# K^T p in four column strips, and the chain's single-column matmuls spread over more slots

## The chip, the cores and the metric

The kernel runs on one core of one Trainium2 chip. The metric is the device time of one execution in microseconds (us). Engines are named as in the profile: PE (TensorE) does the matmuls and PEld its weight loads, DVE is VectorE, ACT is ScalarE, POOL is GpSimd, SP is SyncE, which here only issues loads.

## What is computed

One transformer layer at decode (a single query per sequence, batch 2, width 512), forward and backward. A conditioning vector gives six shift, scale and gate vectors; layer norm, attention over a cache of 8192 keys in 32 heads of 128, then a gated feed-forward block of width 1376. Outputs are the layer's result and the gradients of all inputs but one. The parts that matter for the time:

```python
scores = jnp.einsum('bhqd,bhkd->bhqk', q, k_cache) * Dh ** (-0.5)
p = _softmax(scores, axis=-1)
o = jnp.einsum('bhqk,bhkd->bhqd', p, v_cache)
...
_out, _vjp = jax.vjp(_f, A_x, A_k_cache, A_v_cache, A_wq, A_wo, B_w1, B_w3, B_w2, c, w_mod)
```

K and V are bf16, 2 MB each for each of the 64 (batch, head) pairs. Their gradients are two outer products per head: dV = p dO^T and dK = ds q^T, where ds = p (V dO - sum). Each is 2 MB per head to be written. The gradient of q is the sum over keys of ds times K. The kernel gets it from two things that it collects while K and V are on the chip: the 128x128 matrix V^T diag(p) K, and the vector K^T p. The vector is what the change computes in another way.

## The kernel before

**Two kinds of job.** A job takes eight slots of a schedule that is written out by hand (`at(slot, place, f)`; at the end, all slots are run through in order, and within a slot by place). Jobs of kind A, one for each of 64 heads, load K and V and collect the forward part. Jobs of kind C, one for each head, load V a second time and write dV and dK. C jobs of a batch can only start when the whole batch's A jobs and the chain behind them (output projection, feed-forward, its backward, dO) are through. So A jobs of batch 0 run alone first, 32 of them; then the chain of batch 0 is laid over A jobs of batch 1; then A jobs of batch 1 and C jobs of batch 0 alternate; then come the chain of batch 1 and the rest of the C jobs.

**An A job.** K of a head is two tiles of 1 MB ("half" tiles, 128 partitions x 32 blocks x 128), V as well. In each of eight slots:

- `a_t`: eight 128x128 transposes of K into a PSUM tile `tp` (L353), copied to SBUF by ACT (L358) or, for two of eight groups, by DVE (L356).
- `a_s`, two slots later: eight single-column matmuls of the transposed blocks with q (L373), the scores.
- After eight groups: maximum, exponential (`a_exp`, L391) into `E2`, 64 bf16 values on each partition, each twice.
- `a_scale`, in four parts: DVE multiplies K by p (L399) into `ek`, 128 columns, and POOL puts p itself into a 129th (L401); POOL also keeps p for the C job (L403).
- `a_m`, from slot 15 of the job on (`MOFF`), eight slots: for each of the 64 blocks of 128 keys, one matmul of V with `ek`, 129 columns (L414: V^T diag(p) K and V^T p), and one of K with p, a single column (L416: K^T p). Both accumulate in one PSUM tile, over 64 blocks. K and V are each loaded as weights, 128x128.
- `a_free`: half of K and half of V go back together after four of the eight groups, the others after eight.
- `a_evac`: ACT copies the matrix out, DVE the two vectors into `OK`.

In steady state three A jobs overlap, so a slot holds eight transposes, eight score columns, eight L414 and eight L416.

**A C job.** `c_t` and `c_s` transpose V and multiply with dO (L353 and L951); DVE makes the outer products (L974) into half tiles, which POOL writes out (L979).

**Buffers and loads.** All 1 MB tiles, loads, outputs and large weights, come from one pool of 21. Loads are sorted by the slot that needs them (`want`) and issued on SP in that order, each as soon as a tile is released (`release`, `pump`). SP runs its issues in order, each waiting for its own tile.

**PSUM.** Eight banks: four for `tp`, two for scores and small results (`scr` hands out columns of them), two for L414's sums and other wide results.

**The chain** (`steps_chain`) is a list of steps, each with the number of slots to the next; `lay` puts them on slots as tasks, which come last in a slot. Its matmuls with one column: the output projection (L702, 4 x 32), `proj` for w1 and w3 (L756, 44 each) and w2 (L792, 44). Its 23 slots and the planner's rules set which slot the first C job gets (`TC = E0 + 5`, where `E0` is the end of the chain).

Of the kernel before, what the change touches and what calls it, by code (L numbers as in the profile page):

```python
# [8 lines left out]
BF16 = mybir.dt.bfloat16  # L9
F32 = mybir.dt.float32  # L10
ALU = mybir.AluOpType
ACT = mybir.ActivationFunctionType
AX = mybir.AxisListType
# [4 lines left out]
def kernel(  # L18
# [26 lines left out]
    nc = tc.nc  # L45
    P = 128
    B, Sq, D = A_x.shape
    assert Sq == 1 and B == 2
    _, H, Sk, Dh = A_k_cache.shape
# [3 lines left out]
    NC = D // P  # L53
    KK = Sk // P
    MC = MD // P
    FC = (F + P - 1) // P
    FL = F - (FC - 1) * P
    NHD = B * H
# [8 lines left out]
    HK = KK // 2  # L67
# [4 lines left out]
    def hb(i):  # L72
        return i // H, i % H
# [4 lines left out]
    cst = ctx.enter_context(tc.tile_pool(name="cst", bufs=1))  # L78
# [3 lines left out]
    ktp = ctx.enter_context(tc.tile_pool(name="ktp", bufs=4))  # L82
    ekp = ctx.enter_context(tc.tile_pool(name="ekp", bufs=3))
    hw = ctx.enter_context(tc.tile_pool(name="hw", bufs=2))
    tps = ctx.enter_context(tc.tile_pool(name="tps", bufs=4, space=bass.MemoryType.PSUM))
    sps = ctx.enter_context(tc.tile_pool(name="sps", bufs=2, space=bass.MemoryType.PSUM))
    mps = ctx.enter_context(tc.tile_pool(name="mps", bufs=2, space=bass.MemoryType.PSUM))

    HN = HK * P

# [9 lines left out]
    def mtps():  # L100
        return mps.tile([P, 512], F32, name="m_ps", tag="m_ps")

    identb = cst.tile([P, P], BF16, name="identb")
# [4 lines left out]
    nc.vector.tensor_scalar(nident[:], identb[:], -SCL, None, ALU.mult)  # L108
    eps_t = cst.tile([P, 1], F32, name="eps_t")
    nc.vector.memset(eps_t[:], EPS)  # L110

    rsum = cst.tile([P, NHD], F32, name="rsum")
    OK = cst.tile([P, NHD, 2], F32, name="OK")
# [11 lines left out]
    for nm, ap in (("c", c), ("x", A_x.rearrange("b s d -> (b s) d")),  # L125
                   ("dy", grad_out.rearrange("b s d -> (b s) d"))):
        r = rin[:, len(rows_in), :]
# [21 lines left out]
    K = {}  # L149
# [18 lines left out]
    def kb_(store, i, kk):  # L168
        return store[(i, kk // HK)][:, kk % HK, :]

    def vb_(key, kk):
        return V[(key, kk // HK)][:, kk % HK, :]
# [129 lines left out]
    def at(slot, place, f):  # L302
        seq[0] += 1
        events.setdefault(slot, []).append((place, seq[0], f))

    now = [0]
    PL_EXP, PL_T, PL_X, PL_S, PL_B, PL_MAX, PL_TT, PL_M, PL_FREE, PL_EV, PL_DS, PL_DK, PL_TASK = range(13)
# [4 lines left out]
    def want(need, f):  # L312
        seq[0] += 1
        loads.append((need, seq[0], f))

    def pump():
        while loads and free["half"] - keep[0] >= 1:
            loads.pop(0)[2]()

    def release(n=1):  # L320
        free["half"] += n
# [3 lines left out]
    def head_ps():  # L325
        t = stps()
        cur_ps[:] = [t, now[0], 0]
        return t

    def scr(n):  # L330
        if cur_ps[0] is None or now[0] - cur_ps[1] > 7:
            head_ps()
        if cur_ps[2] + n > 256:
            cur_ps[2] = 0
        o = 256 + cur_ps[2]
        cur_ps[2] += n
        return cur_ps[0][:, o:o + n]

    def pair(ap):
        return ap.rearrange("p k (a b) -> p k a b", b=2)  # L340
# [3 lines left out]
    E2 = {}  # L344
    ek = {}
    kts = {}
    MOFF = NG + LAG + 5
    HG = NG // 2
# [14 lines left out]
    def a_t(i, g):  # L363
        if g == 0:
            S_ps[i] = head_ps()
        kts[(i, g)] = transposes(lambda j: kb_(K, i, g * GRP + j), g in (2, 6))

    def a_s(i, g):
        b, h = hb(i)
        kt = kts.pop((i, g))  # L370
        for j in range(GRP):
            cc = g * GRP + j
            nc.tensor.matmul(S_ps[i][:, cc:cc + 1], kt[:, j, :], qT_bf[:, h, b:b + 1], start=True, stop=True)  # L373
# [21 lines left out]
    def a_scale(i, q):  # L395
        t = ekp.tile([P, QK, 130], BF16, name="ek", tag="ek")
        ks = slice(q * QK, (q + 1) * QK)
        hf, o = divmod(q * QK, HK)
        nc.vector.tensor_tensor(pair(t[:, :, 0:P]), pair(K[(i, hf)][:, o:o + QK, :]),  # L399
                                E2[i][:, ks, :].unsqueeze(2).to_broadcast((P, QK, P // 2, 2)), ALU.mult)  # L400
        nc.gpsimd.tensor_copy(t[:, :, P:P + 1], E2[i][:, ks, 0:1])  # L401
        if q == 0:
            nc.gpsimd.tensor_copy(E["t"][:, i % E["n"], :], E2[i][:, :, 0])  # L403
        ek[(i, q)] = t

    def a_m(i, g):
        if g == 0:
            M_ps[i] = mtps()
        m = M_ps[i]
        q = g * GRP // QK  # L410
        t = ek[(i, q)]
        for j in range(GRP):
            kk = g * GRP + j
            nc.tensor.matmul(m[:, 0:P + 1], vb_(i, kk), t[:, kk % QK, 0:P + 1],  # L414
                             start=(kk == 0), stop=(kk == KK - 1), skip_group_check=True)
            nc.tensor.matmul(m[:, P + 1:P + 2], kb_(K, i, kk), E2[i][:, kk, 0:1],  # L416
                             start=False, stop=(kk == KK - 1), skip_group_check=True)
        if (g + 1) * GRP % QK == 0:
            ek.pop((i, q))

    def a_free(i, g):
        if g % HG == HG - 1:
            K.pop((i, g // HG))
            V.pop((i, g // HG))
            release(2)
        if g == NG - 1:
            E2.pop(i)
        pump()

    def a_evac(i):  # L430
        m = M_ps.pop(i)
        b, h = hb(i)
        nc.scalar.copy(mstate[b][:, h, :], m[:, 0:P])
        nc.vector.tensor_copy(OK[:, i, :], m[:, P:P + 2])

    def job_a(i, s):
        for g in range(NG):
            at(s + g, PL_T, lambda g=g: a_t(i, g))
            at(s + g + LAG, PL_S, lambda g=g: a_s(i, g))
            at(s + g + MOFF, PL_M, lambda g=g: a_m(i, g))  # L440
            at(s + g + MOFF, PL_FREE, lambda g=g: a_free(i, g))
        at(s + NG + LAG, PL_MAX, lambda: a_max(i))
        at(s + NG + LAG + 1, PL_MAX, lambda: a_bias(i))
        at(s + NG + LAG + 2, PL_EXP, lambda: a_exp(i))
        for q in range(NQ):
            at(s + NG + LAG + 3 + 2 * q, PL_TT, lambda q=q: a_scale(i, q))
        at(s + MOFF + NG, PL_EV, lambda: a_evac(i))

    def take_m(b):
# [25 lines left out]
    def load_wo(a):  # L475
        v = hflat()[:].rearrange("p (h d) -> p h d", d=D)
        free["half"] -= 1
        qd.dma_start(v, A_wo.rearrange("(h p) d -> p h d", p=P)[:, a * WH:(a + 1) * WH, :])
        wo_v.append(v)
# [196 lines left out]
    def steps_chain(b):  # L676
        out = []

        def put(n, f):
            out.append((n, f))  # L680

        hold = {}
# [16 lines left out]
        def attn_pe(dc):  # L699
            hold[dc] = scr(1)  # L700
            for h in range(H):
                nc.tensor.matmul(hold[dc], wo_of(h, dc),  # L702
                                 O_bf[:, b, h:h + 1], start=(h == 0), stop=(h == H - 1))
# [1 line left out]
        def attn_ev(dc):  # L705
            nc.vector.tensor_copy(attn[:, dc, b:b + 1], hold[dc])

        put(1, lambda: (attn_pe(0), attn_pe(1)))
        put(0, lambda: (attn_pe(2), attn_pe(3)))
        put(0, lambda: [attn_ev(dc) for dc in range(NC)])  # L710

        def x1_task():
# [35 lines left out]
        put(1, ln_a)  # L748
        put(1, ln_b)

        def proj(nm):
            hold[nm] = scr(FC)
            for fc in range(FC):
                fs = fsz(fc)
                for kc in range(NC):
                    nc.tensor.matmul(hold[nm][:fs, fc:fc + 1], w13_of(nm, kc, fc), h2_bf[:, kc, b:b + 1],  # L756
                                     start=(kc == 0), stop=(kc == NC - 1))

        def proj_ev(nm, dst):
            nc.vector.tensor_copy(dst[:, :FC - 1, b], hold[nm][:, :FC - 1])  # L760
            nc.vector.tensor_copy(dst[:FL, FC - 1, b:b + 1], hold[nm][:FL, FC - 1:FC])

        def p1():
            proj("w1")
            proj_ev("w1", gate)
            hold["e"] = small(FC, "sge", b)
            nc.scalar.activation(hold["e"][:], gate[:, :, b], ACT.Exp, scale=-1.0)

        put(1, p1)

        def p2():
            proj("w3")
            proj_ev("w3", up)

        put(0, p2)

        def p4():
# [6 lines left out]

        put(1, p4)

        def p5():
            hold["f"] = scr(NC)
            for dc in range(NC):
                for fc in range(FC):  # L790
                    fs = fsz(fc)
                    nc.tensor.matmul(hold["f"][:, dc:dc + 1], w2_of(fc)[:, dc * P:(dc + 1) * P],  # L792
                                     hh_bf[:fs, fc, b:b + 1], start=(fc == 0), stop=(fc == FC - 1))
            e = hold["e"]
            nc.vector.tensor_scalar(e[:], hold["sig"][:], -1.0, 1.0, ALU.mult, ALU.add)
            nc.vector.tensor_mul(e[:], e[:], sg[:, :, b])
            nc.vector.tensor_add(dslg[:, :, b], e[:], hold["sig"][:])

        put(0, p5)

        def p6():
# [67 lines left out]
    CS0 = end_a(sA[H - 1]) + 1  # L869
# [4 lines left out]
    s = NG * H  # L874
# [10 lines left out]
    s = max(s, TC)  # L885
# [9 lines left out]
    s = max(s, t1 + 5)  # L895
# [19 lines left out]
    want(FS0 - 3, load_w2)  # L915
    want(CS1, load_w2)
    for a in range(H // WH):
        want(CS0, lambda a=a: load_wo(a))
    for a in range(3):
        want(CS0 + 4, lambda a=a: load_w13(a))  # L920
        want(CS1 + 1, lambda a=a: load_w13(a))
# [83 lines left out]
    for n in range(NHD):  # L1005
        s = sC[n]
# [165 lines left out]
    for kc in range(NC):  # L1172
        for half in range(HD // 2048 if HD >= 2048 else 1):
            w = min(2048, HD)
# [63 lines left out]
    for kc in range(NC):  # L1238
        for m0 in range(0, MD, 2048):
            w = min(2048, MD - m0)  # L1240
# [32 lines left out]
    t = -1  # L1273
# [33 lines left out]
```

## Time and profile before

| | us |
|---|---|
| median of 11 runs | 1809.09 |
| lowest and highest | 1802.91, 1816.59 |
| profiled execution | 1810.75 |
| its span, first to last instruction | 1809.0 |

Busy in the span: PE 1408.3 us (78%), its weight loads 1305.2 (72%), DVE 1180.8 (65%), ACT 955.3 (53%), POOL 362.7 (20%). 718.15 MB are moved, 397 GB/s in the mean; 430 MB are read and 284 MB written.

| group of instructions | count | mean ns |
|---|---|---|
| L353 transposes, PE | 8192 | 250 |
| L414 matmul, 129 columns, PE | 4096 | 218 |
| L416 matmul, 1 column, PE | 4096 | 165 |
| L373 and L951 matmuls, 1 column, PE | 4096 each | 164, 168 |
| L358 copy of a transposed group, ACT | 768 | 1015 |
| L356 copy of a transposed group, DVE | 256 | 687 |
| L399 K times p, DVE | 256 | 1218 |
| L974 outer products, DVE | 512 | 1218 |
| L401 and L403 copies, POOL | 256, 64 | 659, 754 |

How to read it: a group's mean is the length of one instruction. Matmuls are pipelined, so that the lengths of neighbours overlap and the distance of their starts is what one costs. Busy shares are means over stages with different limits; what a stage is worth is read from windows of that stage. The row of clock digits is the clock that PE was granted, in tenths of full speed.

### The profile page before, as it was taken

What the parts mean: (1) busy time and instruction counts of PE and PEld (TensorE: products, weight loads), DVE (VectorE), ACT (ScalarE), POOL (GpSimd) and SP (SyncE); (2) the same over time, 40 slices, a digit from 0 to 9 for tenths busy, and PEclk for the clock granted to TensorE, in tenths of its full rate; (3) what the DMA queues carried; (4) which work ended last, traced back from release to release, by engine and by line L of the source; (5) the groups of instructions that cost most, each with busy time, mean ns of one, the idle gap of its engine ahead of it and who ended that gap; (6) DMA issues with size and microseconds to landing.
All of it is one profiled execution on the core that took longest, in us unless ns stands there. A gap on an engine that the chain in (4) does not pass through costs nothing. (4 is left out here: it accounts for less than half of the span.)

```text
span 1809.0 us, 61208 instructions
## 1 busy us (share of the span) xinstructions
PE 1408.3 (78%) x27266; PEld 1305.2 (72%) x27266; DVE 1180.8 (65%) x1687; ACT 955.3 (53%) x1362; POOL 362.7 (20%) x621
## 2 busy tenths in 40 slices
PE   6888999999987778777777777778768678775862
PEld 5888999999886778676766777777755456564662
DVE  2555555775767666766676667788756566565596
ACT  4555655654454545454555455443465556674662
POOL 0222222331112112212222122111112221111111
PEclk7999999997998888789888888866655556585676
DMA  9999999997899999999999999999999999999997
GB/s 385 418 419 400 386 374 374 379 360 250 331 404 423 418 416 413 407 419 410 412 409 412 408 406 411 400 390 422 416 425 413 404 401 415 405 423 424 416 381 301
DMA packets 115445, 718.15 MB, mean 397 GB/s; under 512 B 11456, under 2 KB 20364, under 8 KB 33260
## 3 DMA queue, kind: packets, MB, share of 16 engines
q1 hardware_dynamic: 73952, 430.01, 60.0%
q0 software_dynamic: 41216, 284.22, 37.8%
q8 instruction: 213, 3.49, 0.7%
q14 instruction: 52, 0.43, 0.1%
q10 hardware_dynamic: 12, 0.01, 0.0%
HBM read 429.99 MB, written 284.20 MB: 395 GB/s over the span
## 5 line engine op out<-in xcount | busy, mean ns | idle before, releaser
L358 ACT COPY kt<-tp 128x1024 bf16<-128x1024 bf16 x768 | 775.4, 1015 | 632.5 <-PE tp L353 621.9
L353 PE MATMUL tp<-identb,half 128*128 128x128 bf16 x8192 | 773.3, 250 | 17.1 <-issue 15.0
L353 PEld LDWEIGHTS <-half 128*128 128x128 bf16 x8192 | 586.9, 112 | 106.3 <-issue 103.3
L974 DVE TENSOR_TENSOR half<-Qr,ds 128x2048 bf16<-128x2048 bf16 x256 | 309.6, 1219 | 195.2 <-DMA out_dram<-half 191.0
L414 PE MATMUL m_ps<-ek,half 128*128 128x129 bf16 x4096 | 411.3, 218 | 14.7 <-POOL ek L401 9.5
L416 PE MATMUL m_ps<-e,half 128*128 128x1 bf16 x4096 | 383.2, 165 | 10.6 <-issue 10.5
L974 DVE TENSOR_TENSOR half<-DOr,e 128x2048 bf16<-128x2048 bf16 x256 | 311.2, 1216 | 115.3 <-DMA out_dram<-half 74.8
L416 PEld LDWEIGHTS <-half 128*128 128x128 bf16 x4096 | 344.2, 96 | 17.2 <-issue 17.2
L414 PEld LDWEIGHTS <-half 128*128 128x128 bf16 x4096 | 346.6, 96 | 11.0 <-issue 10.7
L979 POOL DMA_DIRECT2D out_dram<-half x256 | 136.6, 533 | 996.5 <-DVE half L974 809.5
L399 DVE TENSOR_TENSOR ek<-half,e 128x2048 bf16<-128x2048 bf16 x256 | 308.6, 1218 | 1.8 <-ACT e L391 1.5
L951 PEld LDWEIGHTS <-kt 128*128 128x128 bf16 x4096 | 186.8, 107 | 116.8 <-DVE kt L356 75.5
L951 PE MATMUL s_ps<-DO_bf,kt 128*128 128x1 bf16 x4096 | 191.1, 168 | 101.3 <-DVE kt L356 67.5
L373 PE MATMUL s_ps<-qT_bf,kt 128*128 128x1 bf16 x4096 | 179.0, 164 | 113.9 <-DVE kt L356 100.0
L356 DVE COPY kt<-tp 128x1024 bf16<-128x1024 bf16 x256 | 175.8, 687 | 139.1 <-PE tp L353 137.6
L373 PEld LDWEIGHTS <-kt 128*128 128x128 bf16 x4096 | 160.5, 98 | 121.9 <-DVE kt L356 103.8
L401 POOL COPY ek<-e 128x16 bf16<-128x16 bf16 x256 | 163.8, 659 | 394.0 <-ACT e L391 191.0
L1098 ACT CAST stg<-m_ps 128x512 bf16<-128x512 f32 (+2 forms) x123 | 71.9, 590 | 117.1 <-DMA out_dram<-stg 89.7
L1097 PE MATMUL m_ps<-half 2*128 2x512 bf16 (+2 forms) x123 | 72.3, 588 | 29.4 <-ACT stg L1098 27.7
L403 POOL COPY E<-e 128x64 bf16<-128x64 bf16 x64 | 48.3, 754 | 0.1
L385 DVE TENSOR_REDUCE nm<-s_ps 128x1 f32<-128x128 f32 x64 | 18.4, 287 | 43.1 <-PE s_ps L382 43.1
L391 ACT ACTIVATE e<-s_ps,nm 128x128 bf16<-128x128 f32 x64 | 23.7, 370 | 29.7 <-DVE nm L385 29.6
(219 smaller groups left out, 690.2 us busy)
## 6 DMA issues: line engine op xcount, KB each, us to landing
half<-in_A_v_cache_dram SPq DMA_DIRECT2D x256, 1024.0 KB, 11.0
out_dram<-half POOLq DMA_DIRECT2D x256, 1024.0 KB, 13.0
half<-in_A_k_cache_dram SPq DMA_DIRECT2D x128, 1024.0 KB, 13.8
out_dram<-stg POOLq DMA_DIRECT2D x22, 512.0 KB, 17.6
half<-in_A_wq_dram SPq DMA_DIRECT2D x8, 1024.0 KB, 15.1
half<-in_w_mod_dram SPq DMA_DIRECT2D x6, 1024.0 KB, 14.8
half<-in_B_w_dram SPq DMA_DIRECT2D x6, 1024.0 KB, 15.0
half<-in_A_wo_dram SPq DMA_DIRECT2D x4, 1024.0 KB, 8.7
```

The costliest lines, as they stand in the source:

```text
L353: nc.tensor.transpose(tp[:, j, :], block(j), identb[:])
L356: nc.vector.tensor_copy(kt[:], tp[:])
L358: nc.scalar.copy(kt[:], tp[:])
L373: nc.tensor.matmul(S_ps[i][:, cc:cc + 1], kt[:, j, :], qT_bf[:, h, b:b + 1], start=True, stop=True)
L399: nc.vector.tensor_tensor(pair(t[:, :, 0:P]), pair(K[(i, hf)][:, o:o + QK, :]), E2[i][:, ks, :].unsqueeze(2).to_broadcast((P, QK, P // 2, ...
L401: nc.gpsimd.tensor_copy(t[:, :, P:P + 1], E2[i][:, ks, 0:1])
L414: nc.tensor.matmul(m[:, 0:P + 1], vb_(i, kk), t[:, kk % QK, 0:P + 1], start=(kk == 0), stop=(kk == KK - 1), skip_group_check=True)
L416: nc.tensor.matmul(m[:, P + 1:P + 2], kb_(K, i, kk), E2[i][:, kk, 0:1], start=False, stop=(kk == KK - 1), skip_group_check=True)
L951: nc.tensor.matmul(DP[n][:, cc:cc + 1], kt[:, j, :], DO_bf[:, b, h:h + 1], start=True, stop=True)
L974: nc.vector.tensor_tensor(pair(t[:, o:o + QK, :]), QD[(n, which)][:].rearrange("p (a b) -> p a b", b=2).unsqueeze(1).to_broadcast((P, QK, ...
L979: sq_.dma_start(src_of(dst, n)[:, hf * HK:(hf + 1) * HK, :], t[:])
L1097: nc.tensor.matmul(ps[:lw, 0:rw], rsl(ln, lc, lw), rsl(rn, rc, rw), start=True, stop=True)
```

## The change

- `a_m` loses L416. K^T p is computed by `a_kp`, once per head at slot 17 of its job, as 16 matmuls with p as weights and K as the moving operand: 512 columns, four blocks of K at once. The weights are 32 columns wide: `pz` holds the 64 values per partition in groups of four, each after 28 columns of zeros, and a 32-column window is cut from it so that the four values stand at the four columns of the head in question. Output is one of four strips of 32 PSUM partitions, in turn; each strip sums a quarter of the blocks.
- Eight heads share one PSUM bank (`kps`), each in four of a strip's 32 rows. After eight heads ACT copies the bank out (`a_kp_rows`), and four f32 matmuls with the 0/1 matrix `sel` add up the four strips and pick, for each of the four rows, the 128 columns that belong to it (`a_kp_out`); a DVE copy puts the eight vectors into `OK`.
- `a_pz`: POOL copies the 64 values of p into `pz`, two slots ahead of `a_kp`.
- `kps` takes a PSUM bank from the transposes: `tp` has three buffers, not four.
- K is released apart from V (`k_free`): its first half at slot 17, its second at slot 19, where both went with V at slots 18 and 22.
- The chain's single-column matmuls are spread: the output projection 32 a slot over four slots, not 64 over two; w1, w3 and w2 in two parts each, on slots of their own. The chain is 29 slots long, not 23. By the planner's rules, 39 A jobs stand ahead of the first C job, not 38.
- The loads of `A_wo` are wanted eight slots earlier.

```diff
-    tps = ctx.enter_context(tc.tile_pool(name="tps", bufs=4, space=bass.MemoryType.PSUM))
+    tps = ctx.enter_context(tc.tile_pool(name="tps", bufs=3, space=bass.MemoryType.PSUM))
...
+    kps = ctx.enter_context(tc.tile_pool(name="kps", bufs=1, space=bass.MemoryType.PSUM))
...
+    QP = 4
+    NST = 4
+    NR = P // NST
+    HPB = NR // QP
+    NPG = KK // QP
...
+    sel = cst.tile([P, NR], F32, name="sel")
+    nc.vector.tensor_reduce(sel[:], identb[:].rearrange("p (j x) -> p x j", j=NST), AX.X, ALU.add)
+    pz = cst.tile([P, NPG * NR + NR], BF16, name="pz")
+    nc.vector.memset(pz[:], 0.0)
...
-            nc.tensor.matmul(m[:, P + 1:P + 2], kb_(K, i, kk), E2[i][:, kk, 0:1],
-                             start=False, stop=(kk == KK - 1), skip_group_check=True)
...
+    kp = {}
+
+    def a_pz(i):
+        nc.gpsimd.tensor_copy(pz[:, 0:NPG * NR].rearrange("p (m w) -> p m w", w=NR)[:, :, NR - QP:NR],
+                              E2[i][:, :, 0].rearrange("p (m w) -> p m w", w=QP))
+
+    def a_kp(i):
+        h = i % HPB
+        if h == 0:
+            kp["ps"] = kps.tile([P, QP * P], F32, name="k_ps", tag="k_ps")
+            nc.tensor.matmul(kp["ps"][:, 0:2], identb[:], pz[:, 0:2], start=True, stop=False,
+                             skip_group_check=True)
+        for r in range(NPG // NST):
+            for j in range(NST):
+                m = r * NST + j
+                kk = m * QP
+                o = NR * m + NR - QP - QP * h
+                nc.tensor.matmul(kp["ps"][NR * j:NR * (j + 1), :], pz[:, o:o + NR],
+                                 K[(i, kk // HK)][:, kk % HK:kk % HK + QP, :],
+                                 start=False, stop=(h == HPB - 1 and r == NPG // NST - 1),
+                                 skip_group_check=True)
+
+    def a_kp_rows(i):
+        t = ktp.tile([P, QP * P], F32, name="kprow", tag="kt")
+        nc.scalar.copy(t[:], kp.pop("ps")[:])
+        kp["row"] = t
+
+    def a_kp_out(i):
+        ps = scr(HPB)
+        t = kp.pop("row")
+        for c in range(QP):
+            nc.tensor.matmul(ps, t[:, c * P:(c + 1) * P],
+                             sel[:].rearrange("p (h c) -> p c h", c=QP)[:, c, :],
+                             start=(c == 0), stop=(c == QP - 1))
+        nc.vector.tensor_copy(OK[:, i - HPB + 1:i + 1, 1], ps)
+
+    def k_free(i, hf):
+        K.pop((i, hf))
+        release()
+        pump()
+
     def a_free(i, g):
         if g % HG == HG - 1:
-            K.pop((i, g // HG))
             V.pop((i, g // HG))
-            release(2)
+            release()
...
-        nc.vector.tensor_copy(OK[:, i, :], m[:, P:P + 2])
+        nc.vector.tensor_copy(OK[:, i, 0:1], m[:, P:P + 1])
...
+        at(s + MOFF, PL_EXP, lambda: a_pz(i))
+        at(s + MOFF + 2, PL_T, lambda: a_kp(i))
+        at(s + MOFF + 2, PL_FREE, lambda: k_free(i, 0))
+        at(s + MOFF + 4, PL_FREE, lambda: k_free(i, 1))
+        if i % HPB == HPB - 1:
+            at(s + MOFF + 3, PL_EXP, lambda: a_kp_rows(i))
+            at(s + MOFF + 4, PL_M, lambda: a_kp_out(i))
...
-        put(1, lambda: (attn_pe(0), attn_pe(1)))
-        put(0, lambda: (attn_pe(2), attn_pe(3)))
+        for dc in range(NC):
+            put(1, lambda dc=dc: attn_pe(dc))
...
-        def proj(nm):
-            hold[nm] = scr(FC)
-            for fc in range(FC):
+        def proj(nm, f0, f1):
+            if f0 == 0:
+                hold[nm] = scr(FC)
+            for fc in range(f0, f1):
...
+        FH = (FC + 1) // 2
...
-            proj("w1")
+            proj("w1", FH, FC)
...
+        put(1, lambda: proj("w1", 0, FH))
         put(1, p1)
...
-            proj("w3")
+            proj("w3", FH, FC)
...
+        put(1, lambda: proj("w3", 0, FH))
         put(0, p2)
...
+        put(1, p5a)
         put(0, p5)
...
-        want(CS0, lambda a=a: load_wo(a))
+        want(CS0 - 8, lambda a=a: load_wo(a))
```

`p5a` does the first half of w2's output columns, `p5` the second half and what followed it before.

More of the change, by code (lines that the diff above doesn't have):

```diff
@@ L110 @@
     nc.vector.memset(eps_t[:], EPS)
+    QP = 4
[3 more added lines that the diff above has]
+    NPG = KK // QP
+    assert NHD % HPB == 0 and H % HPB == 0 and NPG % NST == 0
+    sel = cst.tile([P, NR], F32, name="sel")
+    nc.vector.tensor_reduce(sel[:], identb[:].rearrange("p (j x) -> p x j", j=NST), AX.X, ALU.add)
+    pz = cst.tile([P, NPG * NR + NR], BF16, name="pz")
+    nc.vector.memset(pz[:], 0.0)
     rsum = cst.tile([P, NHD], F32, name="rsum")
@@ L785, in steps_chain, with p5a, p5_pe @@
         put(1, p4)
-        def p5():
+        def p5a():
             hold["f"] = scr(NC)
-            for dc in range(NC):
+            p5_pe(0, NC // 2)
+        def p5_pe(d0, d1):
+            for dc in range(d0, d1):
                 for fc in range(FC):
@@ L793, in p5 @@
                                      hh_bf[:fs, fc, b:b + 1], start=(fc == 0), stop=(fc == FC - 1))
+        def p5():
+            p5_pe(NC // 2, NC)
             e = hold["e"]
```

## Prediction

> **What bounds the kernel now.** I read the 40 slices first, to find where bytes flow slower than they can.
>
> ```profile
> PEclk7999999997998888789888888866655556585676
> ...
> GB/s 385 418 419 400 386 374 374 379 360 250 331 404 423 418 416 413 407 419 410 412 409 412 408 406 411 400 390 422 416 425 413 404 401 415 405 423 424 416 381 301
> ```
>
> A slice is 45.2 us. In slices 1 and 2, and from 11 on, some 410 to 420 GB/s are moved; slices 4 to 10 have a dent, deepest (250) where the clock digit falls to 7. The whole kernel moves 718 MB, so only the dent can be won back. The windows view says who sets the pace on either side.
>
> ```profile
> 60.00:150.00 90.00, 77.96 (x1859) 76.16 (x1857) 48.05 (x66) 47.80 (x66) 22.68 (x37) 1.00 1.01 419
> 190.00:410.00 220.00, 207.68 (x4986) 205.32 (x4983) 140.59 (x221) 128.38 (x177) 61.47 (x96) 0.99 0.99 373
> ...
> 510.00:1290.00 780.00, 593.55 (x11895) 575.52 (x11896) 554.13 (x818) 383.88 (x537) 157.62 (x260) 0.82 1.01 411
> 1290.00:1809.00 519.00, 359.72 (x4676) 283.22 (x4673) 333.03 (x363) 300.62 (x456) 88.77 (x162) 0.62 0.98 402
> ```
>
> After each stretch stand the busy times of PE, its weight loads, DVE, ACT and POOL, then clock, DMA share and GB/s. From 510 us on PE is busy 76% and the DMA engines all the time: **DMA sets the pace there**, and less PE work buys nothing. From 190 to 410 us PE is busy 94% and the rate is 373: **PE sets the pace there**; SP's own waits are for PE's matmuls of L416, which free the buffers. Line 414 alone, by stretch, counts heads (64 of its matmuls each):
>
> ```profile
> 60.00:150.00 90.00, 45.81 (x464) 38.78 (x463) 1.00 1.01 419
> 190.00:410.00 220.00, 124.51 (x1240) 104.38 (x1240) 0.99 0.99 373
> ```
>
> 90/(464/64) = 12.4 us a head early, 220/(1240/64) = 11.35 later. A head's K and V are 4.19 MB, 10.0 us at 419 GB/s. So early, too, PE is behind; DMA runs at full rate only because it fills the 21 buffers. One slot of PE's timeline (start, length, what; x8 is a run of eight):
>
> ```profile
> 198.60 0.61 PE L353 MATMUL tp<-identb,half 128*128 128x128 bf16 x8
> 199.04 0.34 PE L373 MATMUL s_ps<-qT_bf,kt 128*128 128x1 bf16 x8
> 199.24 0.22 PE L414 MATMUL m_ps<-ek,half 128*128 128x129 bf16 x1
> 199.30 0.17 PE L416 MATMUL m_ps<-e,half 128*128 128x1 bf16 x1
> 199.33 0.22 PE L414 MATMUL m_ps<-ek,half 128*128 128x129 bf16 x1
> ...
> 199.90 0.61 PE L353 MATMUL tp<-identb,half 128*128 128x128 bf16 x8
> ```
>
> Lengths include a tail that overlaps the next matmul, so starts are what counts: eight transposes 0.44 us (56 ns each), eight score columns 0.20 (25 ns), eight pairs L414 and L416 0.66 (56 + 26 ns). Slot 1.30 us, eight slots **10.4 us a head**. The rest is stalls:
>
> ```profile
> 97.23 0.22 PE L353 MATMUL tp<-identb,half 128*128 128x128 bf16 x1 [0.96 <-issue]
> ```
>
> Early, such a hole of about 1 us comes every 128 matmuls, two a head: 10.4 + 2.0 = 12.4, as counted. The page's instruction queue has 213 packets for PE's 54,532 instructions, 256 (128 loads, 128 matmuls) a packet: I read the holes as a late packet of instructions behind full DMA queues. From 190 on they cost 11.35 - 10.4 = 0.95 a head.
>
> **The K pass.** Out go 64 matmuls of L416, 26 ns each as pace: L414 next to L414 has as many columns as a transpose and one more, so I take its 56 ns. A slot becomes 0.44 + 0.20 + 0.45 = 1.09, a head 8.7 us. In come three things.
>
> 16 matmuls of 512 columns into four 32-column strips. No row has strips side by side. One such matmul alone: L1097's 512-column matmul lasts 384 ns at its shortest, a 128-column one 219 at 56 ns pace, so 384 - 163 = 220 ns. In turn: 16 x 0.22 = 3.5 us; four at a time: 0.88. The ends are far apart and decide the sign, and there the skill has a price: TensorE: Matmul & The Clock Gate, "Measured speedup vs the span model", gives 2.38 times for three column strips of 512 columns, 79% of ideal. Four at 79% are 3.2 times: **1.1 us**, an estimate by that page.
>
> The second rule speaks against it: TensorEngine Tiling, "Key Properties", says that changing the tiling mode drains TensorE. The nearest row is a two-column load among full ones:
>
> ```profile
> 1301.56 0.34 PE L951 MATMUL s_ps<-DO_bf,kt 128*128 128x1 bf16 x8
> 1301.83 0.39 PE L1072 MATMUL m_ps<-identb,O_bf 128*2 128x128 bf16 x4
> 1302.15 0.62 PE L353 MATMUL tp<-identb,half 128*128 128x128 bf16 x8
> ```
>
> Into it 0.27 us where 0.20 is usual, out of it 0.32 where 4 x 0.056 = 0.22: 0.17 us for both switches. The rule gives no time; a full drain of one 219 ns matmul each way would be 0.44. By the row 0.17 a head, by the drain 0.44; I take the row.
>
> Every eighth head, four f32 matmuls: L687 shows one as two records, 0.22 us; 0.9 us per eight heads, 0.11 a head. New base 8.7 + 1.1 + 0.17 + 0.11 = **10.1 us** against 10.4. Instructions fall from 512 to about 416 a head, holes from 2.0 to 1.63. Early: 10.1 + 1.63 = 11.7 against 12.4, 12 heads, -8 us. From 190 to 410: holes stood at 0.47 of their full cost; as DMA is then nearer its 10.0 us, I take 0.55 x 1.63 = 0.9, so 11.0 against 11.35: 19 heads, -7 us. The seven heads around the chain: -2.
>
> **Chain.** Here the clock falls (the third figure from the end of a windows row):
>
> ```profile
> 420.00:430.00 10.00, 9.68 (x223) 9.62 (x220) 4.26 (x17) 2.85 (x4) 0.00 (x0) 0.59 0.75 282
> 430.00:440.00 10.00, 10.00 (x245) 10.00 (x243) 5.68 (x22) 4.78 (x9) 0.83 (x4) 0.67 0.38 129
> 440.00:450.00 10.00, 9.52 (x170) 9.28 (x169) 4.92 (x12) 3.25 (x4) 0.25 (x1) 0.72 0.49 141
> ```
>
> And PE's timeline there:
>
> ```profile
> 419.98 1.74 PE L702 MATMUL s_ps<-O_bf,half 128*128 128x1 bf16 x64
> 421.58 0.92 PE L353 MATMUL tp<-identb,half 128*128 128x128 bf16 x8
> ```
>
> Half clock for 2 x (4.1 + 3.3 + 2.8) = 20 us, though PE is never idle. By the skill's rule (same clock-gate page, "HAM oscillation": no idle gap over about 3.4 us) nothing should throttle here, and spreading the runs would gain 0. The trace differs: the clock changes at 421.7, 432.0, 435.4 and 445.6 us, steps of 3.4; of such windows, by columns streamed per clock, those that kept the full clock had 0.38 and more, those after which it fell at most 0.38; the one from 418.3 us with 64 single columns has 0.21. Transposes then take 0.81 a run for 0.44; about seven such slots lose 0.85 us each and the chain's own transposes the rest: 6.7 us. After: a slot with 32 single columns streams 2056 columns (0.86 us) in 1.09 + 0.83, or 0.45; with 24 in 1.72, 0.50. Both keep the clock, but a 1 us hole in the window brings 0.45 to 0.32. I take **-5** of the 6.7. The same matmuls are issued, so nothing is added on PE; the chain takes 29 slots for 23, and by the planner's rule one more batch-1 head runs before the first output head, at 11.0 us instead of 10.2 (4.19 MB at 411): +1.
>
> **Edits at nothing.** POOL's 64 copies into pz: L403's 128x64 copy is 0.75 us, POOL is 20% busy, and the pass comes two slots (2.2 us) later. POOL takes it in order behind output issues that wait for DVE; PE's L373 already waits for the same DVE (100 us in all), in the DMA-paced part. Without that cover it is 0.75 a head, 24 us over 32 heads. Behind PE's wait for pz stand that slot's score columns and L414, for which ACT's exp would then be late. ACT's eight 128x512 copies (0.59 each at L1098) lie in ACT's waits for transposes. Three transpose buffers: a run needs the copy of three runs ago, and the previous slot's L373 has already needed it; only the chain's slots, with two runs each, are touched: at most one 1.01 us copy in 13 slots, 0 to 13, I take 1. K is freed one and three slots earlier, so SP issues K and V loads earlier; wo's four 1 MB loads move eight slots ahead on SP and hold 4 of 21 buffers longer. SP's loads are behind PE's releases here, so neither decides; if cover is gone, a head's data is late by 4 MB, 10 us once.
>
> **Sum.** -8 - 7 - 2 - 5 + 1 + 1 = -20, uncertain by about 14. The profiled execution took 1810.75 us (span 1809.0); 1791. The median shown, 1809.09, is 1.7 below it: **1789 us**. What is late next in the early part is still PE (11.0 against DMA's 10.0); past 510 us the bytes are unchanged, so the lead is kept.
>
> **Rivals.**
> Ideal strips and no throttle (0.88 us, holes unchanged in share): 9.85 a head; -12 - 11 - 4 - 6.7 = -34, 1775. For it: weight loads already lie beside matmuls (PEld is busy 72% at PE's 78%). It lies in my own range, 1772 to 1800. With the forecast: **0.60**; still lower 0.06.
>
> **Strips in turn, slower.** If matmuls over all 128 rows don't run side by side, the pass is 3.5 us, a head 12.5. Decides above 8.7 + x + 0.28 = 10.4, x = 1.4 us or 89 ns a matmul, less about 0.4 for fewer holes and clock. With holes at 0.3 of 1.63 (DMA less loaded): 13.0 against 11.35 for 26 heads, 14.0 for 12.4 in six, +43 + 10, later heads +11, clock -5: +59, 1868. Past 510 us, PE's 24% idle hides it. For it: no row shows overlap. Against: the page's measured strips. **0.16**, and 0.06 for a milder loss, 1813 to 1850 (switches at full drain, POOL in the path).
>
> **Two at a time, nothing won**: 1.76 us, base 10.75: -1 - 0 - 0 - 5: 1803; or the clock is not kept and the strips are middling, so that the change doesn't do what it is built for: **0.12**, 1800 to 1813.
>
> No change means within 0.2%, 3.6 us, of 1809, about what a measurement of this kernel can tell. Faster: 0.66 and a third of the last case, 0.70; same 0.08; slower 0.22. The range is 1765 to 1830: about 0.03 below, 0.17 above.
>
> **What will show it.** The new pass's 16 matmuls: starts within 1.3 us in all if side by side, 220 ns apart if not; more than 89 ns apart makes me wrong. A slot of 1.09 us; the count of L414's successor from 190 to 410 us near 1280 instead of 1240; clock 1.0 through the chain; the dent at 385 to 395 GB/s; past 510 us, 411 as before. A lower rate there, or PE waiting for POOL's pz, would break the sum too.

## Result, and the profile after

The changed kernel takes 1774.31 us (1769.99 to 1777.43) where the kernel before takes 1808.02 in the same series: ratio 0.9813, 95% interval 0.9795 to 0.9830, 34 us faster. The forecast was 1789, 20 us faster than the 1809 it started from. The profiled execution's span is 1772.0 us against 1809.0.

The page's slices first: granted clock, then GB/s, 44.3 us a slice.

```profile
PEclk9999999989988878888888888575655555575776
...
GB/s 381 417 417 417 418 417 390 417 378 376 364 401 424 420 416 417 405 413 421 414 410 408 409 416 393 422 394 415 424 412 418 400 390 406 377 422 424 420 423 293
```

Slices 1 to 7 (counted from 0) now stand at 417 or 418 but for one; before, slices 4 to 7 had 374 to 386. The dent is left in slices 8 to 10, at 364 to 378: the chain of batch 0. The windows of the stretches (busy PE, PEld, DVE, ACT, POOL, then clock, DMA share, GB/s) say the same:

```profile
60.00:150.00 90.00, 90.00 (x1861) 83.31 (x1858) 57.54 (x82) 56.98 (x80) 33.36 (x53) 1.00 1.01 417
...
410.00:510.00 100.00, 91.92 (x1855) 84.92 (x1856) 72.08 (x135) 52.57 (x75) 22.38 (x48) 0.95 0.98 369
510.00:1290.00 780.00, 582.49 (x10428) 547.11 (x10421) 549.18 (x808) 384.32 (x541) 155.95 (x272) 0.79 1.01 413
```

From 510 us on, DMA moves 413 GB/s at full share, as before (411). The lines of the V^T diag(p) K matmul alone (L427 now) count heads:

```profile
60.00:150.00 90.00, 44.44 (x568) 33.52 (x564) 1.00 1.01 417
190.00:350.00 160.00, 77.18 (x981) 58.27 (x982) 1.00 1.00 410
```

and in the kernel before, L414, the second window:

```profile
190.00:350.00 160.00, 91.41 (x911) 76.75 (x911) 0.99 0.98 376
```

90/(568/64) = 10.1 us a head early and 160/(981/64) = 10.4 up to 350 us, where it was 12.4 and 11.2. PE's timeline with one K pass:

```profile
83.26 0.63 PE L427 MATMUL m_ps<-ek,half 128*128 128x129 bf16 x8
83.82 1.05 PE L449 MATMUL k_ps<-half,pz 128*32 128x512 bf16 x16
84.80 0.62 PE L366 MATMUL tp<-identb,half 128*128 128x128 bf16 x8
```

The pass takes 0.98 us from its first start to the next transposes, and eight L427 in front of it 0.56 where they take 0.47 elsewhere: 1.07 us with the change to 32-column weights in front of it and the change back. Single starts in the trace: the matmuls of four strips start 2 to 5 ns apart, the fours 216 ns apart.

Where the lead was made shows best by bytes. From the DMA records of each trace, the time at which so many MB had been moved (us):

| MB moved | before | after | after, less before |
|---|---|---|---|
| 80 | 198.2 | 195.7 | -2.5 |
| 160 | 412.9 | 394.5 | -18.4 |
| 180 | 482.9 | 447.7 | -35.2 |
| 200 | 536.8 | 500.8 | -36.0 |
| 400 | 1019.6 | 983.9 | -35.7 |
| 700 | 1752.2 | 1716.5 | -35.7 |

All of the lead is there by 180 MB, half of it from the heads before the chain and half across the chain, and little is won or lost after. So two things were to be settled: why the early heads won more than forecast, and whether the second half is the chain edits' work.

### The profile page after: what moved, and what is told of

Read it like the earlier page. It is cut to its first block, busy times and chain, and to the rows that moved or that the text cites. A ratio compares the mean times of both kernels' runs of the same rounds, so it can differ in the third digit from the quotient of the medians.

```text
span 1772.0 us, 55291 instructions
## 1 busy us (share of the span) xinstructions
PE 1391.1 (79%) x24266; PEld 1246.3 (70%) x24266; DVE 1180.5 (67%) x1697; ACT 956.5 (54%) x1370; POOL 386.6 (22%) x685
## 5 line engine op out<-in xcount | busy, mean ns | idle before, releaser
L366 PEld LDWEIGHTS <-half 128*128 128x128 bf16 x8192 | 606.4, 114 | 109.4 <-issue 105.1
L427 PE MATMUL m_ps<-ek,half 128*128 128x129 bf16 x4096 | 326.7, 222 | 9.4 <-DMA half<-in_A_v_cache_dram 7.3
L427 PEld LDWEIGHTS <-half 128*128 128x128 bf16 x4096 | 247.2, 98 | 9.9 <-DMA half<-in_A_v_cache_dram 7.5
L414 POOL COPY ek<-e 128x16 bf16<-128x16 bf16 x256 | 147.1, 594 | 342.5 <-ACT e L404 200.0
L449 PE MATMUL k_ps<-half,pz 128*32 128x512 bf16 x1024 | 67.0, 382 | 19.0 <-POOL pz L435 19.0
L449 PEld LDWEIGHTS <-pz 128*32 128x32 bf16 x1024 | 21.5, 96 | 38.9 <-POOL pz L435 21.2
L416 POOL COPY E<-e 128x64 bf16<-128x64 bf16 x64 | 47.6, 743 | 0.1
L435 POOL COPY pz<-e 128x64 bf16<-128x64 bf16 x64 | 44.9, 702 | 0.0
```

Source lines behind the costliest of these rows:

```text
L366: nc.tensor.transpose(tp[:, j, :], block(j), identb[:])
L449: nc.tensor.matmul(kp["ps"][NR * j:NR * (j + 1), :], pz[:, o:o + NR], K[(i, kk // HK)][:, kk % HK:kk % HK + QP, :], start=False, stop=(h = ...
```

## Experiments

**The parts apart.** The first takes the chain edits out of the changed kernel, the second puts them alone into the kernel before, the third takes back only the place of the wo loads.

```diff
 pass only: after.py
-        for dc in range(NC):
-            put(1, lambda dc=dc: attn_pe(dc))
+        put(1, lambda: (attn_pe(0), attn_pe(1)))
+        put(0, lambda: (attn_pe(2), attn_pe(3)))
...
-        want(CS0 - 8, lambda a=a: load_wo(a))
+        want(CS0, lambda a=a: load_wo(a))
```

(and w1, w3 and w2 each in one part again; the second experiment is the same edit turned round, on the kernel before; the third is its last two lines alone, on the changed kernel)

> The changed kernel with the chain's runs of single columns (64 and 44 a slot), its 23 slots and the wo loads as they were before; the K pass, its PSUM bank and the early release of K stay. Theory 1 (the whole gain is the K pass: heads of batch 0 at 10.1 us instead of 11.7, and the chain edits bring nothing): 1765 to 1776 us. Theory 2 (the sum of the prediction: spreading the runs is worth 5 us): 1779 or more, since the two half-clock stretches of 10 us come back with nothing to cover them.

> The kernel before with only the chain edits: runs of 32 and 20 to 24 single columns, 29 slots, wo loaded eight slots earlier; L416 stays. Theory 1 (chain edits bring nothing): 1804 to 1814 us. Theory 2 (clock kept in the chain, 5 us won): about 1803, with clock 1.0 from 410 to 450 us in the trace.

> The changed kernel with the wo loads wanted at the old slot. Theory 1 (the four early wo loads stand ahead of V of head 32 on SP, and PE's 7.5 us wait for that V, which also halves the clock, is their doing): that wait is gone, 1766 to 1771 us. Theory 2 (DMA sets the pace there anyway, 8 MB of weights have to pass before the chain in either order, the wait only moves): 1772 to 1777 us, with PE waiting for a load of V or of weights somewhere between 360 and 430 us.

Measured, as ratios to the kernel before: pass only 1766.99 us, 0.9780 (0.9767 to 0.9793); chain edits only 1806.67, 0.9997 (0.9985 to 1.0008); wo late 1773.14, 0.9817 (0.9801 to 0.9833). The K pass alone wins 40 us, more than the whole change. The chain edits alone win nothing, and beside the pass they cost 7 us. "Pass only" also has the early release of K, which was not tried apart, so what it adds is open; early on PE is busy for 90.0 of 90 us, and there its own work sets the pace, not the loads. The early wo loads make no difference that these runs can tell (0.9817 without them, 0.9813 with): in the changed kernel PE waits for a V load behind them,

```profile
367.15 0.22 PE L395 MATMUL s_ps<-nident,rm 128*128 128x128 bf16 x1
374.71 1.05 PE L427 MATMUL m_ps<-ek,half 128*128 128x129 bf16 x8 [7.35 <-DMA half<-in_A_v_cache_dram]
```

and with wo late, for wo itself, in the same place:

```profile
379.17 0.35 PE L760 MATMUL s_ps<-O_bf,half 128*128 128x1 bf16 x8 [0.87 <-DMA half<-in_A_wo_dram]
383.69 0.37 PE L760 MATMUL s_ps<-O_bf,half 128*128 128x1 bf16 x8 [4.16 <-DMA half<-in_A_wo_dram]
383.92 1.01 PE L366 MATMUL tp<-identb,half 128*128 128x128 bf16 x8
...
385.81 1.04 PE L760 MATMUL s_ps<-O_bf,half 128*128 128x1 bf16 x32
386.71 1.01 PE L366 MATMUL tp<-identb,half 128*128 128x128 bf16 x8
```

Transposes at 1.01 for 0.62 are those at half clock. The wait only moves; the 8 MB of weights have to pass either way. Pass only has it as well, 6.1 us for wo.

The chain edits alone are not quite the case that the prediction priced: L416 is still in the slot, so a slot with 32 single columns takes 1.30 + 0.83 = 2.13 us and its share of columns is 0.40, not 0.45. In that trace the 3.4 us from 416.8 us, in which PE has no hole, have 0.37, and the clock falls after them.

**Longer chain or shorter runs.** The edits make the chain 29 slots long and cut its runs. Six empty slots give the kernel with the pass alone the length without the cuts.

```diff
 pass only, and at the end of steps_chain:
         put(1, lambda: None)
         put(0, sums)
         put(1, q3)
+        put(6, lambda: None)
```

> The version with the K pass alone (1767 us), its chain's matmuls in runs of 64 and 44 as before, but six empty slots put at the chain's end, so that it is 29 slots long and the planner makes the same order of jobs as in the changed kernel: 39 A jobs before the first C job. Theory 1 (the chain edits cost 7 us because the chain is longer and the first C job a head later): 1772 to 1777 us. Theory 2 (it is the shorter runs themselves, or the loads of wo): 1764 to 1769 us.

1766.13 us, ratio 0.9781 (0.9752 to 0.9810). The longer chain and the planner's other order cost nothing; theory 1 falls. The fair partner is wo late: the same loads, the same 29 slots, the same order of jobs, but spread runs. Its times lie at 1771.3 to 1776.3 us, those of the padded kernel at 1765.3 to 1767.9. So what costs some 7 us are the spread runs, with extra slots between the chain's steps instead of behind them; short runs and the place of the slots were not tried apart. Windows from 380 to 450 us, the changed kernel and then the padded one:

```profile
380.00:450.00 70.00, 63.23 (x1322) 58.96 (x1321) 40.68 (x105) 30.41 (x42) 8.21 (x24) 0.91 0.99 378
```

```profile
380.00:450.00 70.00, 63.11 (x1263) 57.88 (x1264) 40.92 (x105) 28.46 (x40) 7.78 (x24) 0.83 1.01 403
```

The padded one has the lower clock here and moves more bytes, but for a part of the window it is through with its chain and in its empty slots. The same work is compared from the first L427 matmul (L414 before) of head 31 to that of head 39, counted from 0, around the chain. One trace of each kernel; PE's idle times over 0.15 us are sorted by what ended them ("issue" is a hole that no wait explains; POOL and ACT, 1.1 us at most, are left out):

| kernel | eight heads, us | at half clock | idle until DMA | until DVE | until issue |
|---|---|---|---|---|---|
| before | 126.9 | 20.5 | 0 | 3.6 | 6.7 |
| chain edits only | 133.2 | 34.1 | 0 | 5.2 | 6.9 |
| after | 132.2 | 26.3 | 7.8 | 8.9 | 0 |
| wo late | 129.4 | 29.9 | 7.7 | 5.5 | 0 |
| pass only | 128.7 | 27.3 | 6.1 | 7.6 | 0 |
| pass, padded | 124.4 | 23.9 | 6.2 | 5.2 | 0 |

In each pair (before and chain edits only, pass only and after, padded and wo late) the kernel with spread runs takes longer, but the table does not give the cause. Pass only and padded have the same runs and the same time in all, and still differ by 4.3 us here; before and chain only differ by 6.3 us here and by nothing in all. Of the two kernels that differ by the 7 us, after and pass only, the one with the edits has no more time at half clock (26.3 for 27.3) but 3.0 us more of waits; wo late, against padded, has 6.0 us more at half clock and 1.8 us more of waits. How much of the 7 us is clock and how much waits was not separated.

What the traces do show is how the clock is lost. Spread runs keep it while PE has no hole: from 387 to 392.5 us in the changed kernel, with 32 single columns in each slot, it stays at 1.0. Then PE waits for DVE between two steps of the chain:

```profile
393.08 0.94 PE L760 MATMUL s_ps<-O_bf,half 128*128 128x1 bf16 x32
...
396.19 1.02 PE L427 MATMUL m_ps<-ek,half 128*128 128x129 bf16 x8 [1.52 <-DVE both L775]
...
404.20 0.74 PE L815 MATMUL s_ps<-h_bf,half 128*128 128x1 bf16 x24 [1.92 <-DVE h_bf L802]
```

The 3.4 us from 392.5 us, in which the first of these waits begins, have 0.26 of the columns that full clock allows, those from 402.7 us with the second 0.33, and after both the clock is halved. And at half clock such a slot streams too little to get it back at once: with wo late, three windows of 3.4 us from 383.8 us have 0.64 to 0.70 of the columns that half clock allows and stay, and the one with 0.82 that follows returns to full.

**One strip instead of four.**

```diff
-                nc.tensor.matmul(kp["ps"][NR * j:NR * (j + 1), :], pz[:, o:o + NR],
+                nc.tensor.matmul(kp["ps"][0:NR, :], pz[:, o:o + NR],
```

(the copy and the four matmuls at the end then take that strip alone)

> The changed kernel with all 16 matmuls of a K pass going to the first strip of 32 partitions, so that they can't run side by side; the same sums, collected from that strip alone. Theory 1 (side by side is what makes the pass cheap): starts 216 ns apart, a head 10.1 + 16 x 0.216 - 0.9 = 12.6 us with no holes for instructions, 32 heads later by 27 us than in the kernel before, 1830 to 1850 us in all. Theory 2 (the pass is not on the path, DMA sets the pace as soon as L416 is gone): 1774 to 1790 us.

1848.75 us, ratio 1.0231 (1.0210 to 1.0252). A pass now takes 84.51 - 80.95 = 3.56 us,

```profile
80.95 3.63 PE L449 MATMUL k_ps<-half,pz 128*32 128x512 bf16 x16
84.51 0.62 PE L366 MATMUL tp<-identb,half 128*128 128x128 bf16 x8
```

a head 12.6, and the change would have made the kernel slower. Side by side is what decides the sign.

**The holes.** In the changed kernel there is no hole over 0.4 us between 60 and 150 us; the forecast left 1.6 a head. Two kernels change PE's work per instruction: one makes L416 as long as a transpose without a single instruction more, the other puts L416 back beside the K pass.

```diff
 wide column: before.py
-            nc.tensor.matmul(m[:, P + 1:P + 2], kb_(K, i, kk), E2[i][:, kk, 0:1],
+            nc.tensor.matmul(m[:, 2 * P:3 * P], kb_(K, i, kk), E2[i][:, kk, 0:1].to_broadcast((P, P)),
 pass and column: after.py, in a_m
+            nc.tensor.matmul(m[:, P + 1:P + 2], kb_(K, i, kk), E2[i][:, kk, 0:1],
+                             start=False, stop=(kk == KK - 1), skip_group_check=True)
```

> The kernel before with L416's moving operand made 128 columns wide, the same column of p 128 times, so that it takes 56 ns and not 26, with the same number of instructions; one of the columns is kept. Theory 1 (a packet of 256 instructions comes at most every 6.2 us while the DMA queues are full; a hole is what is left of that after the instructions have run): they now run 6.2 us, the holes of 1 us between 60 and 150 us are gone and a head takes 12.3 to 12.5 us there, as before. Theory 2 (each packet costs a hole of about 1 us): 12.3 + 2.0 = 14.3 us a head there.

> The changed kernel with L416 put back beside the K pass (its result is not used; K is released with V's slots as before): 544 instructions a head, 10.1 + 64 x 0.026 = 11.8 us of work. Theory 1 (one packet per 6.2 us): 544/256 x 6.2 = 13.2 us a head between 60 and 150 us. Theory 2 (1 us per packet): 13.9. Theory 3 (holes came from something else that the K pass removed): 11.8.

L414's and L427's counts from 60 to 150 us, first kernel, then second:

```profile
60.00:150.00 90.00, 58.27 (x464) 44.39 (x464) 1.00 1.01 419
```

```profile
60.00:150.00 90.00, 44.44 (x440) 36.94 (x440) 1.00 1.01 411
```

The wide column: 464 matmuls, 12.4 us a head, to the matmul what the kernel before has, and not one hole: 30 ns more in each of 64 matmuls cost nothing there. Pass and column: 440, 13.1 us, with 13 holes of up to 0.9 us. Both are theory 1: at this rate of traffic PE gets 256 instructions per 6.2 us at most, and a hole is what its work leaves of that. That it is the data traffic which delays the packets was not varied. In all they take 1860.77 and 1858.25 us (ratios 1.030 and 1.029): later, where less is moved, the kernel before runs faster than 12.4 us a head and these don't.

**What is late next.** The K pass and what belongs to it left out of "pass only"; K^T p is not computed, zeros stand for it.

> The version with the K pass alone (1767 us), with the pass itself, its POOL copies and its sums left out as well: K^T p is not computed at all (zeros stand for it). PE has 8.7 to 9.0 us of work a head. Theory 1 (with the pass, PE and DMA are level: DMA's 10.0 us a head is next, so that a free K^T p would buy almost nothing more): heads between 60 and 150 us at 10.0 us, at most 6 us less in all, 1760 to 1767. Theory 2 (PE still sets the pace with the pass, by its 10.1 us): heads under 10 us and 1750 or less.

1762.13 us, ratio 0.9743 (0.9722 to 0.9765), 5 us below pass only. From 60 to 150 us,

```profile
60.00:150.00 90.00, 83.21 (x1736) 80.55 (x1734) 58.37 (x82) 58.63 (x81) 27.57 (x46) 1.00 1.01 417
```

PE is busy 83 us where it was 90, the rate is the same 417 GB/s, and from 90 to 283 us heads come at 10.2 us, where pass only has 10.3. With the K pass PE and DMA are level, and so are its instructions (416 of them at 6.2 us for 256 are 10.1 us); a free K^T p would buy 5 us more.

**Three transpose buffers**, in the kernel before (`bufs=4` to `bufs=3`):

> The kernel before with three transpose buffers in PSUM instead of four. Theory 1 (the third-last copy is always needed earlier by the score columns): no change, 1804 to 1811 us. Theory 2 (chain slots with two transposed groups wait for a copy): 1812 to 1822 us.

1808.52 us, ratio 1.0008 (0.9986 to 1.0029): nothing, theory 1.

## Why the prediction was right, and where its sum was not

- **The sum is closer than its terms.** The pass was put at 17 us (8 + 7 + 2) and wins 40 alone; the chain edits were put at 5 won and 1 lost, and cost 7. The two misses have opposite signs, and that 34 came of a forecast of 20 owes something to luck. So does the likeness to the rival of ideal strips, 34 us too: 7 of these were for the clock.
- **What bounds the kernel**: right. PE set the pace before the chain, DMA after 510 us; the lead of 36 us at 200 MB is 36 us at 700 MB.
- **K pass, 1.1 us and 0.17 for the switches**: right in kind, 1.07 for both together where the sum had 1.27. The switches show as 0.09 us in front and 0.10 behind, near the row that was taken; a full drain at 0.44 is not seen. The price that the Trainium skill gives for three strips (TensorE: Matmul & The Clock Gate, "Measured speedup vs the span model", 2.38 times) was on the high side when carried over to four, 1.1 us for 0.98: 16 starts within 0.67 us are four streams of 216 ns, practically ideal. The rival of strips in turn was priced at 3.5 us a pass, 12.5 a head and 1868 us; with one strip 3.56, 12.6 and 1848.75.
- **A head's base, 10.1 us**: right (10.1 measured; a slot is 1.11 for 1.09, since L427 next to L427 starts every 59 ns, not 56).
- **Holes, "from 2.0 to 1.63" a head**: this term was mis-sized, and with it the early -8 us and the -7 up to 410. I took a hole as the price of a packet of instructions. It is the rest of a fixed 6.2 us: before, 256 instructions ran in 5.2 and left 1.0; with the pass they run about 6.2 (10.1 x 256/416) and leave nothing. Early heads went from 12.4 to 10.1, not to 11.7: 12 heads, -27 us. Up to 350 us they came at 10.4, not at the 11.0 of the sum. The sign that was named, near 1280 matmuls from 190 to 410 us, did not come: 1206, because the chain with its waits had moved into that stretch.
- **Chain, "I take -5"**: this step failed. Its edits win nothing alone (ratio 0.9997) and cost 7 us beside the pass, and the sign that was named, clock 1.0 through the chain, did not come: 26.3 us at half clock around it in the changed kernel and 34.1 with the edits alone, for 20.5 before. The count of columns was right for a slot at full clock without a hole. The prediction named a hole of 1 us as what would break it, and gave that too little weight: PE waits inside the chain for what each step needs, and with the pass, which brings it there earlier, for 8 MB of weights too. Half clock followed such waits, and at half clock the same slot stays below the share that brings it back. Why this ends 7 us worse than the old runs stays open: the time at half clock does not account for it (26.3 us in the changed kernel, 27.3 with the pass only).
- **The half of the lead across the chain** (18 to 35 us between 160 and 180 MB) is thus the pass's as well: pass only has it too, 443.5 us at 180 MB. PE came to the chain 43 us earlier (head 31 at 361.6 for 405.1 us) with less read ahead (147 MB moved, not 157), and before, the lead in bytes had been spent there: 184 GB/s from 420 to 450 us.
- **Edits at nothing**: right for the three buffers (1.0008). wo's loads eight slots earlier were put at nothing: PE waited 7.35 us for a V load behind them, but without the edit it waits 5.0 us for wo, and the time is the same within the intervals. PE did wait for POOL's pz, 19.0 us in all, but 17.9 of them after 510 us, where DMA sets the pace and PE waits 100 us for DVE as well. The longer chain was put at +1; padding shows 0.

The version that beats both kernels is the pass without the chain edits: 1767 us, 7 below the changed kernel.

## What to carry to other kernels

Many small matmuls over one tensor can be turned round, so that the tensor streams and the small operand is the weight; in four column strips that costs a quarter of its streaming time, and the sign of the change hangs on the four going side by side, which one edit to a single strip tests. Where DMA is saturated, count PE's instructions as well as its columns: less work in a packet of 256 bought nothing here below 6.2 us, so fewer, longer matmuls can win on both counts. And before single columns are spread to save the clock, see in the trace what PE waits for there: here the spread runs kept the clock only while PE had no hole, and won nothing in the whole.

## What the runs showed that was not expected

- Instructions as a limit. The trace's instruction queue moves 16 KB packets; between 60 and 150 us in the kernel before one starts every 6.2 us and takes 1.07, and each hole ends 2.3 to 2.6 us after such a start. The rate of 256 instructions in 6.2 us fits four kernels (in the trace of the chain edits alone it is 6.0): 12.4 us a head for 512 instructions, without (before) and with (wide column) 30 ns more in each L416; 13.1 for 544; and no hole at 416 in 10.1.
- Four strips that each stream their own 512 columns cost no more than one: 0.98 us a pass for 3.56 in one strip, 3.6 times, and the 16 starts lie within 0.67 us in all of the 64 passes.
- The clock goes with a count of columns. In the kernel before, by windows of 3.4 us: the 41 windows at full clock after which it fell have 0.38 or less of the columns that full clock allows, the 256 after which it stayed have 0.38 or more. Of the windows at half clock, those after which it returned have 0.72 or more of what half clock allows, those after which it stayed low 0.82 or less. In columns these are nearly one number, since 0.75 of half clock is 0.38 of full, about 3100 columns (8100 fit at the 216 ns per 512 of the K pass). So it looks like one mark and not two: a slot that meets it at full clock can miss it at half, because it then takes longer. Slots with 32 single columns did: 0.43 at full clock (the changed kernel from 389.0 us), 0.64 to 0.70 of half clock, or 0.32 to 0.35 of full, with wo late. Idleness alone is not the mark: in the kernel before, PE has no hole in the 3.4 us from 432.0 us, with 0.34 of the columns, and the clock fell after them.
